# Attention units reordered and paced over half outputs, and one more q through the crossbar, in a sparse-attention and bilinear-FFN kernel

## The chip, the cores and the metric

One core of one Trainium2 chip. The metric is device time in microseconds (us) of one execution. Six runs of the kernel before gave a median of 247.2 us, from 246.9 to 249.48. The profile is of one execution, which took 247.11 us; the span from its first to its last instruction is 245.3 us.

## The reference

Per head, an 8x8 matrix is normalised five times over rows and columns, mixes the eight blocks of k and of v, and each block of q then attends to its own mixed block. The result, with heads side by side, goes through a bilinear FFN.

```python
B, H, S, D = 4, 8, 768, 64          # n_blocks 8, block 96
for _ in range(5):
    P = P - np.max(P, axis=-1, keepdims=True)
    P = np.exp(P)
    P = P / (np.sum(P, axis=-1, keepdims=True) + 1e-09)
    P = P / (np.sum(P, axis=-2, keepdims=True) + 1e-09)
k_sorted = np.einsum('bhij,bhjcd->bhicd', P, k_b)
v_sorted = np.einsum('bhij,bhjcd->bhicd', P, v_b)
scores = scale * q_b @ k_sb.transpose(0, 1, 2, 4, 3)
attn = softmax(scores)
x = (attn @ v_sb).transpose(0, 2, 1, 3).reshape(3072, 512)
out = ((x @ w_a) * (x @ w_b)) @ w_out      # w_a, w_b: 512 x 1536, w_out: 1536 x 512
```

All inputs and the output are float32; the kernel computes in bf16 with float32 sums.

## The kernel before

**Tiling.** Heads go in pairs; pair g = 4*b + hp, so batch b has pairs 4b to 4b+3. A pair's work is a set of units:

- `c_` (a mix unit): where q isn't brought in by the crossbar, `turn_q` (L255) transposes it with 12 matmuls and a copy by DVE; `stage_mix` (L274) mixes k and v, 12 matmuls each, into a two-bank PSUM tile, and copies them to SBUF: kT by two ACT copies, vT by one of DVE and one of ACT. For pairs above the first of batch 1, a DMA transpose on SP's queue then turns vT into vs (L292). For pairs 6 to 13 the unit also issues, on POOL, a tiny `gate` copy that waits for kT (L533) and the three loads of pair g+2 (L95).
- `s_` (a score unit): `stage_scores` (L295), 16 matmuls in two PSUM tiles, each followed by an exp on ACT.
- `o_` (an output unit): `stage_o` (L310), 16 matmuls in two PSUM tiles, each followed on DVE by a reciprocal and a multiply; `to_xT` (L316) then sends the result through a DMA transpose on SP into xT, the FFN's input. It also asks for q of pair g+2: a POOL copy that reorders it (`pair_q`, L244) and a DMA transpose on SP (`stage_q`, L250).

The FFN of a batch is 24 pairs of products (`ffn_ab`, L340: 4 matmuls with w_a, 4 with w_b, an ACT cast and a DVE multiply), 12 for each half of the tokens, and 6 output tiles (`ffn_out`, L368: 12 matmuls, a copy by ACT or DVE, a store on SP).

**Stages.** Sinkhorn's steps run first, on DVE and ACT, while POOL issues loads. Then the first half of batch 0's attention (`half_*` functions) runs alone; the second half is interleaved with the first half of batch 0's FFN. After that, `paced` (L567) interleaves the FFN of batch b with the attention units of batch b+1; the last batch's FFN runs alone. PE, POOL and SP run in program order as written, and so do ACT and DVE in the first stage.

**Pacing.** `paced` runs the FFN's steps and after each issues the units that have fallen due. A pair of products counts 1, an output tile 2; the units are spread evenly up to `spare` output tiles before the end (3 in batch 0, 2 otherwise). Batch 0's FFN has 12 pairs left by then, the others 24.

**Places the change touches.** PSUM is 8 banks: `psA` (L67) has two buffers of two banks, for mixes, scores and o; `psF` (L68) has four of one bank, for FFN tiles and transposes. `replicate` (L434) copies the normalised matrix to `p_rep`, half by DVE and half by POOL; `to_columns` (L439) then turns each half into PSUM columns by matmuls. `begun` (L481) holds the five FFN products of batch 0 started before the last quarter of their input is there: three in psF tiles and two in the halves of one psA tile, `two`. `pair_q(2 * HP - 1)` (L499) reorders q of batch 1's fourth pair; `spread` behind it makes the mixing matrices of batches 2 and 3, also on POOL.

Of the kernel before, what the change touches and what calls it, by code (L numbers as in the profile page):

```python
# [9 lines left out]
FP32 = mybir.dt.float32  # L10
# [6 lines left out]
def _ap(t: bass.AP, extra_offset, pattern):  # L17
    return bass.AP(tensor=t.tensor, offset=t.offset + extra_offset,
                   ap=[list(p) for p in pattern])
# [3 lines left out]
def kernel(  # L23
# [11 lines left out]
    nc = tc.nc  # L35
    P = 128
    B, H, S, D = q.shape
    NB = sort_net.shape[-1]
    BLK = S // NB
    BH = B * H  # L40
    DMODEL = H * D
# [3 lines left out]
    CG = P // NB  # L45
    NCH = S // P
    HP = H // 2
    KA = DMODEL // P
    KO = DFF // P
# [17 lines left out]
    psA = ctx.enter_context(tc.tile_pool(name="psA", bufs=2, space=PSUM))  # L67
    psF = ctx.enter_context(tc.tile_pool(name="psF", bufs=4, space=PSUM))  # L68
# [19 lines left out]
    def load_pair(b, hp):  # L88
        tiles = []
        for name, t in (("k2", k), ("v2", v), ("q2", q)):  # L90
            base = (b * H + 2 * hp) * S * D
            if b == 0 and name == "q2":
                continue
            to = ld.tile([P, 2, W], BF16, tag=name, name=name)
            nc.gpsimd.dma_start(out=to, in_=_ap(t, base, [[W, P], [S * D, 2], [1, W]]))  # L95
            tiles.append(to)
        loaded[b * HP + hp] = tiles
# [3 lines left out]
    w_out_sb = const.tile([P, KO, DMODEL], BF16, name="w_out_sb")  # L101
# [8 lines left out]
    def load_out(c):  # L110
        nc.gpsimd.dma_start(
            out=w_out_sb[:, c * 4:(c + 1) * 4, :],
            in_=moe_w_out.rearrange("(kc p) n -> p kc n", p=P)[:, c * 4:(c + 1) * 4, :])
# [46 lines left out]
    def copy(eng, out, in_):  # L160
        if eng == "act":
            nc.scalar.copy(out=out, in_=in_)  # L162
        else:
            nc.vector.tensor_copy(out=out, in_=in_)  # L164
# [79 lines left out]
    def pair_q(g):  # L244
        qc = qtp.tile([P, NCH, 2, D], BF16, tag="qc", name="qc", bufs=4)
        nc.gpsimd.tensor_copy(out=qc.rearrange("p c e d -> p e c d"),  # L246
                              in_=loaded[g][2].rearrange("p e (c d) -> p e c d", c=NCH))
        st[g, "qc"] = qc

    def stage_q(g):  # L250
        qT = qtp.tile([P, NCH, P], BF16, tag="qTf", name="qTf", bufs=4)
        nc.sync.dma_start_transpose(out=qT, in_=st[g, "qc"].rearrange("p c e d -> p (c e d)"))
        st[g, "qT"] = qT
# [69 lines left out]
    hTs = {}  # L323
# [32 lines left out]
    def ffn_last(b, c):  # L356
        hT = hTs[b]
        rows = out[b * S:(b + 1) * S, :].rearrange("(p c) n -> c p n", c=NCH)
        for n0, n1, eng, queue in ((0, 384, "act", nc.sync), (384, DMODEL, "dve", nc.scalar)):
            po = psF.tile([P, 512], FP32, tag="F", name="po")  # L360
            for m in range(KO):
                nc.tensor.matmul(po[:, 0:n1 - n0], lhsT=hT[:, m, c * P:(c + 1) * P],  # L362
                                 rhs=w_out_sb[:, m, n0:n1], start=(m == 0), stop=(m == KO - 1))
            o_sb = ffp.tile([P, 512], FP32, tag="o_sb", name="o_sb", bufs=3)
            copy(eng, o_sb[:, 0:n1 - n0], po[:, 0:n1 - n0])
            queue.dma_start(out=rows[c][:, n0:n1], in_=o_sb[:, 0:n1 - n0])

    def ffn_out(b, c):  # L368
        if b == B - 1 and c == NCH - 1:
            ffn_last(b, c)  # L370
            return
        hT = hTs[b]
        po = psF.tile([P, DMODEL], FP32, tag="F", name="po")
        for m in range(KO):
            nc.tensor.matmul(po, lhsT=hT[:, m, c * P:(c + 1) * P], rhs=w_out_sb[:, m, :],  # L375
                             start=(m == 0), stop=(m == KO - 1))
        o_sb = ffp.tile([P, DMODEL], FP32, tag="o_sb", name="o_sb", bufs=3)
        copy("act" if c % 2 == 0 else "dve", o_sb, po)
        if b == 0:
            h, u = divmod(c, 3)  # L380
            for c2 in range(2):
                nc.sync.dma_start(
                    out=_ap(out, (h * PH * NCH + 2 * u + c2) * DMODEL,
                            [[NCH * DMODEL, PH], [1, DMODEL]]),
                    in_=o_sb[c2 * PH:(c2 + 1) * PH])
        else:
            rows = out[b * S:(b + 1) * S, :].rearrange("(p c) n -> c p n", c=NCH)
            nc.sync.dma_start(out=rows[c], in_=o_sb)


    with tc.manual_schedule(engines={ET.PE, ET.Pool, ET.SP}):
        with tc.manual_schedule(engines={ET.Activation, ET.DVE}):
            rsum = const.tile([BH, NB], FP32, name="rsum")
            csum = const.tile([BH, NB], FP32, name="csum")
            p_fin = const.tile([BH, NB * NB], FP32, name="p_fin")
            p_rep = const.tile([BH, NB * NB, CG // 2], FP32, name="p_rep")
# [3 lines left out]
            for it in range(5):  # L400
# [8 lines left out]
                if it == 2:  # L409
                    with nc.allow_low_precision("sum of one one and zeros"):  # L410
                        nc.vector.reduce_sum(
                            out=mask, in_=_ap(ident, 0, [[P, P], [1, CG], [CG, NB]]),
# [3 lines left out]
                if it > 0:  # L416
                    nc.tensor.matmul(heat[0:NB, 1, 0:NB], lhsT=rsum, rhs=rsum,
                                     start=True, stop=True)
# [8 lines left out]
                else:  # L427
                    nc.vector.tensor_mul(
                        out=p_fin.bitcast(BF16).rearrange("h (i j u) -> h i j u", i=NB, j=NB),
                        in0=_ap(p_nat, 0, [[NB * NB, BH], [NB, NB], [1, NB], [0, 2]]),  # L430
                        in1=_ap(csum, 0, [[NB, BH], [0, NB], [1, NB], [0, 2]]))
            NR = NBH * NB

            def replicate(eng, hf):  # L434
                eng.tensor_copy(
                    out=p_rep[:, hf * NR:(hf + 1) * NR],
                    in_=_ap(p_fin, hf * NR, [[NB * NB, BH], [1, NR], [0, CG // 2]]))

            def to_columns(hf):  # L439
                for i in range(hf * NBH, (hf + 1) * NBH):  # L440
                    nc.tensor.matmul(
                        pc_ps[:, i, :],
                        lhsT=p_rep[:, i * NB:(i + 1) * NB].bitcast(BF16).rearrange(
                            "h j t -> h (j t)"),
                        rhs=ident[0:BH, 0:BH], start=True, stop=True)

            replicate(nc.vector, 0)
            replicate(nc.gpsimd, 1)
            to_columns(0)
            spread(nc.vector, pc_ps, 0, 2, 0, NBH)  # L450
            spread(nc.vector, pc_ps, 2, 6, 0, NBH)
# [27 lines left out]
            half_x(0, 2, "act")  # L479
            half_o(0, 3)  # L480
            begun = [psF.tile([P, 512], FP32, tag="F", name="pf") for _ in range(3)]  # L481
            two = psA.tile([P, 2, 512], FP32, tag="A", name="two")
            begun += [two[:, 0], two[:, 1]]
            for n, (m, w_sb) in enumerate(((0, w_a_sb), (0, w_b_sb), (1, w_a_sb),
                                           (1, w_b_sb), (2, w_a_sb))):
                if n == 3:
# [9 lines left out]
        load_pair(1, 3)  # L496
        for c in range(3):
            load_out(c)
        pair_q(2 * HP - 1)  # L499
        for g in range(2, 4):  # L500
            spread(nc.gpsimd, p_col, g * 8, 8)
# [22 lines left out]
        def units_full(b):  # L524
            g0, us = b * HP, []

            def c_(g):
                if g < 2 * HP - 1:
                    turn_q(g)
                stage_mix(g, "k", ("act",))  # L530
                stage_mix(g, "v", ("dve", "act"))
                if 2 * HP - 2 <= g < B * HP - 2:
                    nc.gpsimd.tensor_copy(out=gate, in_=kTs[g % NBUF][0:1, 0:1])  # L533
                    load_pair((g + 2) // HP, (g + 2) % HP)

            def s_(g):
                stage_scores(g)
                if g == HP:
                    turn_v(g)
                if g == HP + 1:  # L540
                    stage_q(2 * HP - 1)

            def o_(g):
                stage_o(g)
                to_xT(g)
                if 2 * HP <= g + 2 < B * HP:
                    pair_q(g + 2)
                    stage_q(g + 2)

            for n in range(HP + 1):  # L550
                if n < HP:
                    us.append(lambda g=g0 + n: c_(g))
                    us.append(lambda g=g0 + n: s_(g))
                if n > 0:
                    us.append(lambda g=g0 + n - 1: o_(g))
            return us

        def interleave(steps, units, spare, slow=0):
# [6 lines left out]
                    done += 1  # L565

        def paced(ab, po, units, spare):  # L567
            steps = [(1, f) for f in ab] + [(2, f) for f in po]
            total = sum(t for t, f in steps) - 2 * spare
            now = done = 0  # L570
            for t, step in steps:
                step()
                now += t
                while done < len(units) and done * total < now * len(units):
                    units[done]()
                    done += 1

        steps = [lambda: ffn_ab(0, 0, 0, begun[0:2]), lambda: ffn_ab(0, 1, 0, begun[2:4]),
                 lambda: ffn_ab(0, 2, 0, begun[4:5])]
# [3 lines left out]
        for b in range(B):  # L583
            ab = [lambda m=m, t=t, b=b: ffn_ab(b, m, t)
                  for m in range(KO) for t in range(2) if b > 0 or t == 1]
            po = [lambda c=c, b=b: ffn_out(b, c) for c in range(NCH)]
            paced(ab, po, units_full(b + 1) if b + 1 < B else [], 3 if b == 0 else 2)


# [28 lines left out]
```

The softmax here doesn't subtract the row's maximum and nothing guards it: scores larger than these inputs give would overflow.

## Time and profile before

| what | value |
|---|---|
| median of 6 runs | 247.2 us |
| the profiled execution | 247.11 us |
| its span | 245.3 us |
| granted TensorE clock | 1.00 |
| first pf of batch 0, 1, 2, 3 (FFN) | 21.5, 86.6, 141.1, 195.7 us |
| matmuls of 128x384 into pf (L332) | 760, 77.8 + 77.4 us busy |
| output matmuls of 128x512 (L375) | 60.5 us busy |
| bytes moved | 27.82 MB, about 200 GB/s to 50 us, mean 113 |

Times in the trace are from the span's start. Engines are PE (matmuls), PEld (weight loads, which overlap), DVE, ACT, POOL and SP; a line such as L332 is the line of the kernel. Where an engine sat idle before an instruction, square brackets give how long and what ended the wait. In the chain that ended last, the work is followed back from the last instruction, at each step to what released it. Some matmul records are missing, so a group may count 11 where 12 ran.

### The profile page before, as it was taken

Reading aid. Unit: us, or ns where it says so; the run is one execution under the profiler, and the core shown is the slowest. Engines: PE = TensorE matmul, PEld = TensorE weight load, DVE = VectorE, ACT = ScalarE, POOL = GpSimd, SP = SyncE. Lnnn points to the kernel's source line nnn. Section 1 sums busy time; section 2 is a strip of 40 time slices with the busy share of each in tenths; the row PEclk is TensorE's granted clock in tenths of the full one; section 3 lists DMA queues with packets and bytes.
Section 4 is the critical chain, followed back from the end, with each engine's and each line's share of the span. In section 5 each row is a group of like instructions: output and inputs, shape, how many; then the busy total and the mean of one; then the engine's idle time right before and its main releaser. Section 6 shows DMA issues by size and latency. Waiting matters only on the chain.

```text
span 245.3 us, 5508 instructions
## 1 busy us (share of the span) xinstructions
PE 236.6 (96%) x2246; PEld 137.4 (56%) x2258; DVE 109.2 (45%) x259; ACT 104.1 (42%) x203; POOL 61.0 (25%) x88
## 2 busy tenths in 40 slices
PE   7889899999989999999999999999999999999995
PEld 2466666666644456666645466666645465565443
DVE  6765466556425243464616144454516144443210
ACT  3565764465650046555440055555540033333001
POOL 8885577700332031314141032210000000000000
DMA  6999999946959968939393936935333310000122
GB/s 80 202 199 197 197 200 201 207 76 78 156 96 213 144 134 131 139 68 139 67 168 103 214 73 112 139 65 45 64 90 118 118 45 0 0 3 1 43 106 108
DMA packets 53129, 27.82 MB, mean 113 GB/s; under 512 B 29936, under 2 KB 50160, under 8 KB 53104
## 3 DMA queue, kind: packets, MB, share of 16 engines
q0 software_dynamic: 20944, 14.16, 40.9%
q1 hardware_dynamic: 32016, 13.25, 24.8%
q8 instruction: 17, 0.28, 0.5%
q14 instruction: 8, 0.07, 0.1%
q10 hardware_dynamic: 144, 0.07, 0.1%
HBM read 28.32 MB, written 6.29 MB: 141 GB/s over the span
## 4 chain that ended last, share of the span: by engine, by line
PE 91%; DMA 2%; POOL 2%; DVE 2%; issue 1%; ACT 0%
PE pf L332 51%; PE po L375 24%; PE mix L281 4%; PE o_ps L231 3%; DMA q_first<-in_q_dram 2%; PE sc L302 2%; PE mixh L180 2%; PE po L362 1%; PE vs_ps L208 1%; PE xt_ps L222 1%; PE sc L195 1%; POOL w_b_sb L106 1%; POOL w_a_sb L106 1%; PE two L332 1%; PE q_ps L260 1%
## 5 line engine op out<-in xcount | busy, mean ns | idle before, releaser
L353 DVE TENSOR_TENSOR hT<-a_sb,pf 128x384 bf16<-128x384 bf16 x95 | 52.6, 553 | 73.6 <-PE pf L332 48.5
L332 PE MATMUL pf<-xT,w_a_sb 128*128 128x384 bf16 x380 | 77.8, 326 | 0.0
L332 PE MATMUL pf<-xT,w_b_sb 128*128 128x384 bf16 x380 | 77.4, 326 | 0.0
L352 ACT CAST a_sb<-pf 128x384 bf16<-128x384 f32 x95 | 45.5, 479 | 62.1 <-PE pf L332 40.8
L375 PE MATMUL po<-w_out_sb,hT 128*128 128x512 bf16 x265 | 60.5, 379 | 0.7 <-issue 0.2
L332 PEld LDWEIGHTS <-w_b_sb 128*128 128x128 bf16 x384 | 37.5, 98 | 25.2 <-issue 0.6
L332 PEld LDWEIGHTS <-w_a_sb 128*128 128x128 bf16 x384 | 34.9, 98 | 22.2
L375 PEld LDWEIGHTS <-hT 128*128 128x128 bf16 x276 | 26.3, 98 | 30.3
L162 ACT COPY o_sb<-po 128x512 f32<-128x512 f32 (+1 forms) x13 | 7.5, 578 | 50.3 <-PE po L375 48.9
L164 DVE COPY o_sb<-po 128x512 f32<-128x512 f32 (+1 forms) x12 | 7.9, 658 | 44.3 <-PE po L375 38.7
L307 ACT ACTIVATE eT<-sc 96x768 bf16<-96x768 f32 x24 | 18.1, 803 | 3.2 <-PE sc L302 3.2
L533 POOL COPY gate<-kT 1x1 bf16<-1x1 bf16 x8 | 1.4, 179 | 69.5 <-ACT kT L162 69.5
L237 DVE TENSOR_TENSOR xp<-o_ps,rec 96x512 bf16<-96x512 f32 x24 | 15.7, 683 | 0.2
L162 ACT CAST kT<-mix 128x384 bf16<-128x384 f32 x24 | 10.3, 483 | 8.1 <-PE mix L281 8.1
L95 POOL DMA_DIRECT2D k<-in_k_dram x16 | 11.6, 726 | 5.0 <-PE pf L332 2.0
L95 POOL DMA_DIRECT2D v<-in_v_dram x16 | 11.5, 721 | 2.5 <-DMA w_b_sb<-in_moe_w_b_dram 0.8
L231 PEld LDWEIGHTS <-eT 96*128 96x128 bf16 x256 | 10.3, 97 | 3.1 <-issue 0.6
L246 POOL COPY qc<-q 128x768 bf16<-128x768 bf16 x9 | 7.6, 841 | 16.1 <-DMA q<-in_q_dram 16.1
L231 PE MATMUL o_ps<-vs,eT 96*128 96x65 bf16 x256 | 11.2, 193 | 0.1
L95 POOL DMA_DIRECT2D q<-in_q_dram x12 | 8.7, 723 | 1.6 <-DMA w_a_sb<-in_moe_w_a_dram 0.7
L168 PE MATMUL heat<-warm 128*128 128x512 bf16 x20 | 7.1, 491 | 1.4 <-DVE warm L77 1.3
L164 DVE CAST vT<-mix 128x384 bf16<-128x384 f32 x12 | 6.7, 558 | 3.9 <-PE mix L281 3.8
(80 smaller groups left out, 153.6 us busy)
## 6 DMA issues: line engine op xcount, KB each, us to landing
out_dram<-o_sb SPq DMA_DIRECT2D x17, 256.0 KB, 2.0
k<-in_k_dram POOLq DMA_DIRECT2D x16, 192.0 KB, 5.0
v<-in_v_dram POOLq DMA_DIRECT2D x16, 192.0 KB, 6.1
q<-in_q_dram POOLq DMA_DIRECT2D x12, 192.0 KB, 6.0
w_a_sb<-in_moe_w_a_dram POOLq DMA_DIRECT2D x6, 256.0 KB, 10.4
w_b_sb<-in_moe_w_b_dram POOLq DMA_DIRECT2D x6, 256.0 KB, 10.1
w_out_sb<-in_moe_w_out_dram POOLq DMA_DIRECT2D x3, 512.0 KB, 10.0
out_dram<-o_sb SPq DMA_DIRECT2D x12, 128.0 KB, 2.4
```

The source lines that it names most:

```text
L95: nc.gpsimd.dma_start(out=to, in_=_ap(t, base, [[W, P], [S * D, 2], [1, W]]))
L162: nc.scalar.copy(out=out, in_=in_)
L164: nc.vector.tensor_copy(out=out, in_=in_)
L231: nc.tensor.matmul(o_ps[:, e, i * (D + 1):(i + 1) * (D + 1)], lhsT=eT[:, hf, e, i * BLK:i * BLK + P], rhs=vs[0:BLK, i0 + i, V0 - 1 + e * ( ...
L237: nc.vector.tensor_tensor(out=_ap(xp, i0 * 2 * D, [[nxp * 2 * D, BLK], [D, 2], [2 * D, NBH], [1, D]]), in0=_ap(o_ps, 1, [[1024, BLK], [511 ...
L246: nc.gpsimd.tensor_copy(out=qc.rearrange("p c e d -> p e c d"), in_=loaded[g][2].rearrange("p e (c d) -> p e c d", c=NCH))
L281: nc.tensor.matmul(mix[e * D:(e + 1) * D, c // 3, c % 3 * P:(c % 3 + 1) * P], lhsT=src2[:, e, c * D:(c + 1) * D], rhs=s_all[:, 2 * g + e], ...
L307: nc.scalar.activation(out=eT[:, hf, :, 0:HB], in_=sc[0:BLK, :, 0:HB], func=AF.Exp, scale=float(scale))
L332: nc.tensor.matmul(pf[:, 0:HW], lhsT=w_sb[:, kc, m * P:(m + 1) * P], rhs=x_cols(b, kc, t), start=(kc == 0), stop=(kc == KA - 1))
L352: nc.scalar.copy(out=a_sb, in_=pf[:, 0:HW])
L353: nc.vector.tensor_mul(out=hT[:, m, t * HW:(t + 1) * HW], in0=a_sb, in1=ab[1][:, 0:HW])
L375: nc.tensor.matmul(po, lhsT=hT[:, m, c * P:(c + 1) * P], rhs=w_out_sb[:, m, :], start=(m == 0), stop=(m == KO - 1))
```

## The change

It has five parts. The second half of `p_rep` is copied by ACT in place of POOL. The two products of `begun` that shared the tile `two` get a tile each. In `paced`, output tiles are cut into two steps of 6 matmuls each, and all steps count 1. The units of a batch come in a new order, in which the third and fourth mix stand one unit sooner, before the first and second output unit:

```
before: c0 s0 c1 s1 o0 c2 s2 o1 c3 s3 o2 o3
after:  c0 s0 c1 s1 c2 o0 s2 c3 o1 s3 o2 o3
```

And q of batch 1's third pair (g = 6) goes through POOL's reordering and the crossbar, not through matmuls; with it, q of the pairs from 8 on is asked for in the score unit of the pair before, where the output unit of the second pair before did it.

```diff
--- before.py
+++ after.py
@@ -367,13 +367,21 @@
 
     def ffn_out(b, c):
         if b == B - 1 and c == NCH - 1:
-            ffn_last(b, c)
-            return
-        hT = hTs[b]
-        po = psF.tile([P, DMODEL], FP32, tag="F", name="po")
-        for m in range(KO):
-            nc.tensor.matmul(po, lhsT=hT[:, m, c * P:(c + 1) * P], rhs=w_out_sb[:, m, :],
-                             start=(m == 0), stop=(m == KO - 1))
+            return [lambda: ffn_last(b, c)]
+        held = {}
+
+        def part(n):
+            if n == 0:
+                held["po"] = psF.tile([P, DMODEL], FP32, tag="F", name="po")
+            for m in range(n * KO // 2, (n + 1) * KO // 2):
+                nc.tensor.matmul(held["po"], lhsT=hTs[b][:, m, c * P:(c + 1) * P],
+                                 rhs=w_out_sb[:, m, :], start=(m == 0), stop=(m == KO - 1))
+            if n == 1:
+                store(b, c, held["po"])
+
+        return [lambda: part(0), lambda: part(1)]
+
+    def store(b, c, po):
         o_sb = ffp.tile([P, DMODEL], FP32, tag="o_sb", name="o_sb", bufs=3)
         copy("act" if c % 2 == 0 else "dve", o_sb, po)
         if b == 0:
@@ -432,9 +440,8 @@
             NR = NBH * NB
 
             def replicate(eng, hf):
-                eng.tensor_copy(
-                    out=p_rep[:, hf * NR:(hf + 1) * NR],
-                    in_=_ap(p_fin, hf * NR, [[NB * NB, BH], [1, NR], [0, CG // 2]]))
+                copy(eng, p_rep[:, hf * NR:(hf + 1) * NR],
+                     _ap(p_fin, hf * NR, [[NB * NB, BH], [1, NR], [0, CG // 2]]))
 
             def to_columns(hf):
                 for i in range(hf * NBH, (hf + 1) * NBH):
@@ -444,8 +451,8 @@
                             "h j t -> h (j t)"),
                         rhs=ident[0:BH, 0:BH], start=True, stop=True)
 
-            replicate(nc.vector, 0)
-            replicate(nc.gpsimd, 1)
+            replicate("dve", 0)
+            replicate("act", 1)
             to_columns(0)
             spread(nc.vector, pc_ps, 0, 2, 0, NBH)
             spread(nc.vector, pc_ps, 2, 6, 0, NBH)
@@ -479,8 +486,7 @@
             half_x(0, 2, "act")
             half_o(0, 3)
             begun = [psF.tile([P, 512], FP32, tag="F", name="pf") for _ in range(3)]
-            two = psA.tile([P, 2, 512], FP32, tag="A", name="two")
-            begun += [two[:, 0], two[:, 1]]
+            begun += [psA.tile([P, 2, 512], FP32, tag="A", name="two")[:, 0] for _ in range(2)]
             for n, (m, w_sb) in enumerate(((0, w_a_sb), (0, w_b_sb), (1, w_a_sb),
                                            (1, w_b_sb), (2, w_a_sb))):
                 if n == 3:
@@ -496,6 +502,7 @@
         load_pair(1, 3)
         for c in range(3):
             load_out(c)
+        pair_q(2 * HP - 2)
         pair_q(2 * HP - 1)
         for g in range(2, 4):
             spread(nc.gpsimd, p_col, g * 8, 8)
@@ -525,7 +532,7 @@
             g0, us = b * HP, []
 
             def c_(g):
-                if g < 2 * HP - 1:
+                if g < 2 * HP - 2:
                     turn_q(g)
                 stage_mix(g, "k", ("act",))
                 stage_mix(g, "v", ("dve", "act"))
@@ -537,22 +544,19 @@
                 stage_scores(g)
                 if g == HP:
                     turn_v(g)
-                if g == HP + 1:
-                    stage_q(2 * HP - 1)
+                if g in (HP, HP + 1):
+                    stage_q(g + 2)
+                if 2 * HP <= g + 1 < B * HP:
+                    pair_q(g + 1)
+                    stage_q(g + 1)
 
             def o_(g):
                 stage_o(g)
                 to_xT(g)
-                if 2 * HP <= g + 2 < B * HP:
-                    pair_q(g + 2)
-                    stage_q(g + 2)
-
-            for n in range(HP + 1):
-                if n < HP:
-                    us.append(lambda g=g0 + n: c_(g))
-                    us.append(lambda g=g0 + n: s_(g))
-                if n > 0:
-                    us.append(lambda g=g0 + n - 1: o_(g))
+
+            for u, n in ((c_, 0), (s_, 0), (c_, 1), (s_, 1), (c_, 2), (o_, 0), (s_, 2), (c_, 3),
+                         (o_, 1), (s_, 3), (o_, 2), (o_, 3)):
+                us.append(lambda u=u, g=g0 + n: u(g))
             return us
 
         def interleave(steps, units, spare, slow=0):
@@ -565,12 +569,11 @@
                     done += 1
 
         def paced(ab, po, units, spare):
-            steps = [(1, f) for f in ab] + [(2, f) for f in po]
-            total = sum(t for t, f in steps) - 2 * spare
-            now = done = 0
-            for t, step in steps:
+            steps = ab + po
+            total = len(steps) - 2 * spare
+            done = 0
+            for now, step in enumerate(steps, 1):
                 step()
-                now += t
                 while done < len(units) and done * total < now * len(units):
                     units[done]()
                     done += 1
@@ -583,7 +586,7 @@
         for b in range(B):
             ab = [lambda m=m, t=t, b=b: ffn_ab(b, m, t)
                   for m in range(KO) for t in range(2) if b > 0 or t == 1]
-            po = [lambda c=c, b=b: ffn_out(b, c) for c in range(NCH)]
+            po = [f for c in range(NCH) for f in ffn_out(b, c)]
             paced(ab, po, units_full(b + 1) if b + 1 < B else [], 3 if b == 0 else 2)
 
 
```

## The prediction

> **What bounds the kernel now.** I read the page first: busy times, the chain, the groups.
>
> ```profile
> PE 236.6 (96%) x2246; PEld 137.4 (56%) x2258; DVE 109.2 (45%) x259; ACT 104.1 (42%) x203; POOL 61.0 (25%) x88
> ```
>
> PE is busy for 236.6 of 245.3 us, no other engine for half of it, and the chain that ended last is 91% PE. The granted clock is 1.00 in every 5 us window, so PE time falls only by taking matmuls away or by closing gaps. The gaps are 245.3 - 236.6 = 8.7 us. The chain in order of time (start, length, what) shows which can be closed:
>
> ```profile
> 13.13 0.41 POOL p_rep L435
> 13.54 0.04 issue
> 13.59 0.26 PE pc_ps L441 x4
> ...
> 26.33 0.55 DVE hT L353
> 26.87 0.04 issue
> 26.91 0.32 PE two L332
> ...
> 59.89 0.46 PE q_ps L260 x12
> 60.35 0.67 PE mix L281 x24
> ...
> 69.96 0.81 PE mix L281 x24
> 70.80 0.57 DVE vT L164
> 71.39 0.49 ACT vT L162
> 71.88 0.04 issue
> 71.92 0.35 PE sc L302 x8
> 72.26 0.16 issue
> ...
> 87.90 0.79 PE mix L281 x24
> ```
>
> Three places lie off PE inside the body: PE waits for a POOL copy at 13.5, for a DVE multiply at 26.3, and for copies of a mix at 70.8. The rest of the 8.7 us is the first copies, Sinkhorn's serial steps and the last store, which the change leaves alone. The timeline has the first gap from both sides:
>
> ```profile
> 11.21 0.28 DVE L435 COPY p_rep<-p_fin 32x256 f32<-32x256 f32 x1
> ...
> 13.59 0.26 PE L441 MATMUL pc_ps<-ident,p_rep 32*128 32x32 bf16 x4 [0.83 <-POOL p_rep L435]
> ```
>
> DVE copied its half at 11.21; POOL, first in issuing weight loads, reached the other half at 13.13. The reader should see that p_fin had been ready since 11.18.
>
> **Part 1: second half of p_rep from POOL to ACT.** ACT's queue ahead of it is two qT copies, over at 11.13. Its nearest copies by size are 0.26 us (32x64 exp) and 0.48 us (128x384 cast), so this one ends by 11.18 + 0.48 = 11.7. Behind it on ACT stands the kT cast, which started at 12.60. PE wants the data after the v half-mix, 13.59 - 0.83 = 12.76. The whole 0.83 us goes, if nothing is late next. Next are: the heads 2 to 7 of s_all (DVE ready 12.60, wanted 13.0), kT (13.08, wanted 13.3), vT (13.35, wanted 13.6), p_col behind vT (13.35 + 0.42 = 13.8, then the vs copy at 14.0). Pairs of k and v land about 1 us apart; POOL's next issues, which wait for those landings, put v2 before 15.07 (its half-mix would come at 16.66 - 0.83 = 15.83) and k3 before 15.80 (16.47). All hold, with 0.2 us at the narrowest, so I take 0.80; bounds 0.5 (one of the narrow ones is 0.3 late) to 0.83.
>
> **Part 2: "two" as two tiles.** The last matmul into the second half waited 0.61 us until DVE had read the first half: one tile, two banks. With two tiles that reader is no longer waited for. Price: both psA buffers are held. The second takes the buffer of the last o_ps, which DVE has read by 22.61 with PE there at 23.6 (and the xph transposes between wait for the same DVE work anyway). The next sc takes the first one's buffer, free at 26.87, wanted at 27.89 - 0.61 = 27.28. What is late next is ACT's a_sb of that step, behind two casts until 27.07 instead of 27.27; four psF buffers cover it. I take 0.58; bounds 0.4 to 0.61.
>
> **Part 3: q of pair 6 by the crossbar.** Off PE go 12 transposes, off DVE one qT copy of 0.55, which hid behind PE. With q_ps ahead, q_ps and mix take 0.46 + 0.67 = 1.13; the mix of a pair without them takes 0.79 (87.90). So 0.34 us, not 0.46; bounds 0.34 and 0.46. Added: one POOL copy (mean 0.84) ahead of pair 7's copy and two spreads. It waits for q of pair 6, and pair 7's copy, behind it, waited 3.49 us for its own later load until 44.76, which hides it; without that cover the spreads end 0.84 later than 49.5 and are first needed at 87.9. On SP it adds a transpose (1.24 to issue, median 2.8 to landing) at about 42 to 46, wanted at 63. Cost zero.
>
> A rule here. The trace has 12 transposes in 0.46 us, 0.04 each. "TensorE: Matmul & The Clock Gate" (Part 4, PE-mode transpose) gives about 275 ns for one in a kernel. By that, my estimate of this part would be 12 x 0.275 = 3.3 us and the forecast some 3 us lower; the row decides against it.
>
> **Part 4: units over output halves.** In batch 0's FFN the steps are 12 pairs and then 12 half outputs (before, 6 outputs that count 2), and the 12 units are spread over the first 18, so they fall due past 0, 1.5, 3, ... steps. Before, the fourth mix and its scores both fell due after the first output tile: PE went mix, wait, scores. After, the mix comes at step 11, scores at 14, half an output past the first half, so its three casts (kT twice, vT) are hidden by 3.9 us of matmuls. The stage from 67.37 to 86.60 is 19.23 us; its work is 6 outputs x 2.59 (67.37 to 69.96) + mix 0.79 + scores 0.45 + two o units x 0.49 = 17.76. Excess 1.47 us. What may come back: the last o (step 17) follows the one before (step 16) by one half output, 1.29 us, and DVE must first copy the second output. Before, from that output's end (74.96) DVE was through both halves of the first o at 77.11, 2.15 us later. The second half of the last o would want its buffer at 0.49 + 1.29 + 0.25 = 2.03. So 0.2 us with latency. Its vs by the crossbar: from the end of the mix to the last o I add 1.41 + 1.29 + 0.49 + 1.29 + 0.45 + 2.59 + 0.49 + 1.29 = 9.3 us; against it 1.1 to 1.6 for the casts and 3.0 to 6.4 to land:
>
> ```profile
> vs<-vT SPq DMA_TRANSPOSE x11, 5.6
> ```
>
> That is 8.0 at worst. I take 1.47 - 0.2 = 1.27; bounds 0.65 (only the longest stall goes) and 1.47.
>
> A rule against this part. All windows have clock 1.00, also where units stand between FFN steps. The same page ("Why this matters for your kernels") wants all K-tiles of a thin product run together, lest the clock oscillate. By it, an estimate: the six halved outputs of one batch at half clock would cost 6 x 2.59 = 15.5 us more. But units put matmuls, no idle time, between the halves.
>
> **Part 5: mixes one unit sooner in batches 2 and 3, q later.** Before, these stages had no gap (86.60 to 195.66 is PE piece on piece), so there is nothing to win. The third and fourth mix go from steps 14 and 22 to 11 and 19; o 0 and 1 from 11 and 19 to 14 and 22; the last o stays at 30, so xT lands as before. With each mix go its gate and three loads on POOL and the vs transpose on SP, all earlier and so safer. q of pair g+1 is now asked for at scores g, one (mix, scores) ahead where it was two. Tightest is pair 9: gate to 89.2, loads to 92.43, copy 0.85 gives 93.3, landing 2.8 (most 4.5) gives 96.1 (97.8); scores start at 100.65. On SP it stands behind vs of pair 8, issued at 89.83. Zero, with bounds 0.1 gained and 0.6 lost.
>
> **The sum.** 0.80 + 0.58 + 0.34 + 1.27 = 2.99. Profiled span 245.3 - 3.0 = 242.3; around it lie 247.11 - 245.3 = 1.81, giving 244.1. The profiled run is 0.09 under the median 247.2, so against the median 244.2. I say 244.1. The lower bounds sum to 0.5 + 0.4 + 0.34 + 0.65 - 0.6 = 1.3 (245.9), the upper to 0.83 + 0.61 + 0.46 + 1.47 + 0.1 = 3.5 (243.7).
>
> **Rivals.**
> A: the forecast, 244.1, chance 0.70, its own range 243.6 to 245.2.
> B: the early gains are swallowed, since to 50 us the loads run at a steady 200 GB/s and PE can't outrun them. Then only 0.34 + 1.27 count: 245.6. For it: the DMA row is full there. Against: no wait of PE on a load stands in the chain after 13.6. Chance 0.12.
> C: the change moves the wait. psA has two buffers; close o units or scores wait for DVE or ACT, and part 4 gives back its 1.27 and some of the early parts: about 246.3. For it: the last o is now one half behind its neighbour. Against: 0.2 by the rows. Chance 0.10.
> D: slower. The q transposes on SP's in-order queue, asked for late, arrive after their scores are due. Place: scores of pairs 9 and 13, six steps after the request. From q landing 100.65 - 93.3 = 7.4 us after its copy, each microsecond more stalls PE fully, twice. To lose 3.0 and another 1.3 each must be 2.15 late, a landing of 9.5 us: 248.5 and up. For it: vs landed after up to 6.4 us. Against: q never over 4.5. Chance 0.08.
>
> **The numbers.** A kernel like this tells about 0.5% from no change: 1.24 us, so faster is under 245.96. A and B are faster but for a tail of 0.04 where their losses add up: 0.78; C and that tail same, 0.14; D 0.08. Range: 243.5, past A's upper bounds, to 246.0, which takes in B and leaves out D and most of C.
>
> **What would show it.** Right: PE's wait on p_rep is gone from the list of waits, "two" waits for no hT, the sequence mix, vT, scores is gone and the stage from the first output to the next batch's first pf is near 17.9 us, with 12 q_ps fewer. Wrong: a wait of scores on qTf, of o_ps on vs or xp, of pf on weights, or pieces in batches 2 and 3 longer than 54.5 us from one batch's first pf to the next (86.60 to 141.13).

## The result and the profile after

| | before, beside it | after |
|---|---|---|
| median | 247.91 us (49 runs, 246.86 to 253.39) | 246.06 us (23 runs, 245.52 to 246.60) |
| ratio, 95% interval | | 0.9929 [0.9911, 0.9947] |
| profiled execution | 247.11 us | 246.82 us |
| its span | 245.3 us | 245.1 us |

The kernel is 0.71% faster (0.53 to 0.89). That is about 1.75 us of 247.8, where 3.0 were forecast. Before's median of 247.91 stands above the 247.2 shown earlier because 19 of its 49 executions took 249 us or more, and the ratio leaves out only the longest of these: the median of the other 30 is 247.24 us, 1.18 above after's.

The profiled execution of after is the longest of its kernel (other spans: 243.7 to 244.8). The changed kernel was run again as the first experiment, with a span of 244.3 us, and where one execution's luck matters I read that one too.

The page of after has the engines' busy times, and PE's list of waits, from its second line on, has the total in us, the count and the longest:

```profile
PE 237.0 (97%) x2234; PEld 137.2 (56%) x2246; DVE 109.4 (45%) x258; ACT 104.5 (43%) x204; POOL 61.3 (25%) x88
```

```profile
PE sc L195 <- issue: 0.9, 1, 0.9
PE pc_ps L448 <- DVE p_rep L164: 0.5, 1, 0.5
...
PE o_ps L231 <- DVE xp L237: 0.2, 1, 0.2
```

The waits that the change was to remove are gone: no wait on POOL's p_rep, none of "two" on hT, none of scores on vT. PE has 12 matmuls fewer. But the line of scores on "issue" is new. Scores of the first stage wait 0.9 us for nothing that the profile shows. The chain of after, in order of time (start, length, what), has the three places of the prediction and the last copy:

```profile
18.16 0.23 PE sc L195 x6
18.39 0.87 issue
19.26 0.22 PE sc L195 x2
...
26.79 0.50 PE mixh L180 x24
27.29 0.27 PE two L332
...
70.84 0.29 PE sc L302 x8
71.15 0.34 PE sc L302 x8
...
85.89 1.30 PE pf L332 x8
...
241.74 0.29 DVE o_sb L164
```

PE stops in the middle of 8 matmuls whose operands are there: six run, two come 0.87 us later. "two" follows the mixes at once. The four-step jam of mix, vT, scores at 70 is gone. And from the end of DVE's last copy, at 242.03, to the end of the span is 3.1 us; before, it was 242.75 to 245.3, 2.55:

```profile
242.46 0.29 DVE o_sb L164
```

### The profile page after: what moved, and what is told of

Same layout as the page of the kernel before. It is cut to its first block, busy times and chain, and to the rows that moved or that the text cites. A ratio compares the mean times of both kernels' runs of the same rounds, so it can differ in the third digit from the quotient of the medians.

```text
span 245.1 us, 5487 instructions
## 1 busy us (share of the span) xinstructions
PE 237.0 (97%) x2234; PEld 137.2 (56%) x2246; DVE 109.4 (45%) x258; ACT 104.5 (43%) x204; POOL 61.3 (25%) x88
## 4 chain that ended last, share of the span: by engine, by line
PE 92%; DVE 4%; issue 1%; ACT 1%; DMA 1%
PE pf L332 51%; PE po L377 24%; PE mix L281 4%; PE o_ps L231 3%; PE sc L302 2%; PE mixh L180 2%; PE po L362 1%; PE vs_ps L208 1%; PE sc L195 1%; PE xt_ps L222 1%; PE heat L168 1%; DMA p_nat<-in_sort_net_dram 1%; PE q_ps L260 1%; PE two L332 1%; DVE xp L237 1%
## 5 line engine op out<-in xcount | busy, mean ns | idle before, releaser
L377 PE MATMUL po<-w_out_sb,hT 128*128 128x512 bf16 x265 | 61.3, 379 | 0.6
L237 DVE TENSOR_TENSOR xp<-o_ps,rec 96x512 bf16<-96x512 f32 x24 | 15.9, 684 | 0.6 <-DVE rec L235 0.2
L235 DVE RECIPROCAL rec<-o_ps 96x8 f32<-96x8 f32 x32 | 5.6, 189 | 13.8 <-PE o_ps L231 13.8
L246 POOL COPY qc<-q 128x768 bf16<-128x768 bf16 x10 | 8.4, 840 | 7.5 <-DMA q<-in_q_dram 7.5
L168 PE MATMUL heat<-warm 128*128 128x512 bf16 x20 | 7.7, 529 | 1.4 <-DVE warm L77 1.3
```

Of the source, the lines that this page charges most:

```text
L168: nc.tensor.matmul(ps[:, 0:cols], lhsT=warm[:, 0:P], rhs=warm[:, 0:cols], start=True, stop=True)
L237: nc.vector.tensor_tensor(out=_ap(xp, i0 * 2 * D, [[nxp * 2 * D, BLK], [D, 2], [2 * D, NBH], [1, D]]), in0=_ap(o_ps, 1, [[1024, BLK], [511 ...
L377: nc.tensor.matmul(held["po"], lhsT=hTs[b][:, m, c * P:(c + 1) * P], rhs=w_out_sb[:, m, :], start=(m == 0), stop=(m == KO - 1))
```

## The experiments

Every kernel was run beside the kernel before. Medians of five or more runs, ratios with 95% intervals. There are three groups of four experiments, in the order below, with medians of the kernel before of 247.46, 247.54 and 247.62 us. The change itself ran only in the first, so a later median is set against it across groups, and a difference of 0.1 to 0.2 us says nothing.

**The change again.**

> The changed kernel once more. Theory F: the 0.87 us gap of PE in the middle of the half scores of pair 2 (18.39 in the first profile) is PE waiting for its next block of instructions, asked for a fixed number of instructions earlier while the loads fill the DMA engines; it comes back in every execution, 0.6 to 1.1 us long, in the same place. Rival R: it is an accident of one execution, and the part on p_rep really gave its 0.8; then the gap is gone here, and the time is about 245.3. The start (p_fin at 11.18 before, 11.83 after) may differ by half a us from execution to execution under both.

Measured: 245.91 us, ratio 0.9932 [0.9908, 0.9956], span 244.3. Its chain:

```profile
12.94 0.19 PE pc_ps L448 x4
...
17.40 0.23 PE sc L195 x6
17.64 0.87 issue
18.51 0.22 PE sc L195 x2
```

The gap comes again, of the same size, after the same six matmuls, though everything here runs 0.75 us earlier than in the first profile. So it is neither luck nor a fixed time; it sits at a fixed place in PE's program. In the trace of after, 222 matmuls and 224 weight loads lie ahead of the two that come late. The DMA queue's rows name a candidate. In the stretch from 16 to 17 us of this execution (packets, MB, share of the 16 engines):

```profile
q0 software_dynamic: 371, 0.18, 136.2%
q8 instruction: 1, 0.02, 5.9%
```

One packet of instructions, among 371 packets of loads; it is the first of its queue in the span. Over the whole span there are 17 such packets with 0.28 MB, 16 KB each.

**Undo the first part: p_rep's second half on POOL again.**

> The changed kernel with the second half of p_rep on POOL again. F: PE waits about 0.8 us for p_rep again, between the request for the block and its use, so the gap in the scores of pair 2 goes and the time stays within 0.3 us of the changed kernel. R: no gap in either, the wait comes back alone, 0.6 to 0.9 us slower.

```diff
-            replicate("act", 1)
+            nc.gpsimd.tensor_copy(out=p_rep[:, NR:2 * NR],
+                in_=_ap(p_fin, NR, [[NB * NB, BH], [1, NR], [0, CG // 2]]))
```

Measured: 245.85 us, 0.9931 [0.9902, 0.9961], span 244.1: no different from the change. Its timeline, with the idle time before an instruction in brackets:

```profile
13.14 0.41 POOL L455 COPY p_rep<-p_fin 32x256 f32<-32x256 f32 x1
...
13.61 0.26 PE L448 MATMUL pc_ps<-ident,p_rep 32*128 32x32 bf16 x4 [0.63 <-DVE vT L164]
...
18.07 0.37 PE L195 MATMUL sc<-qT,kT 64*128 64x96 bf16 x8
```

The wait at 13.6 is back (the last to release it shows as vT; POOL's copy ended 0.06 us before) and the gap at 18 is gone: the eight scores run in one piece. The first part of the change moves a wait, it removes none.

**Move the border of PE's instructions.** If PE waits for a block of instructions, the block should be asked for sooner when PE is further on in its program at the same time. Warming matmuls of 512 columns were cut into two of 256: same PE time, 21 matmuls and 21 weight loads more ahead of the gap. The same edit to the kernel before is the control.

> The changed kernel with the warming matmuls of the start cut in two (256 columns, twice as many): about 42 more PE instructions (21 pairs) ahead of the same work, the same columns. F: the block's border moves 42 instructions up the program, its request falls into the wait for Sinkhorn and comes 1 to 2 us sooner; the gap of 0.87 goes or falls under 0.2, 0.6 to 0.9 us faster than the changed kernel. R: no difference beyond 0.2 us, or slower by the added weight loads.

> The kernel before with the same 42 more instructions, as a control. F: no gap was left in it (the block arrived 0.1 us ahead of its use), so the time is that of the kernel before within 0.2 us. R: the same; should the added instructions themselves cost or bring something, it shows here.

```diff
-            keep_busy(heat[:, 0], 8)
+            keep_busy(heat[:, 0], 16, 256)
...
-                    keep_busy(heat[:, 0], (0, 4, 3, 2, 4)[it])
+                    keep_busy(heat[:, 0], (0, 8, 6, 4, 8)[it], 256)
```

Measured: in after, 245.02 us, 0.9887 [0.9845, 0.9928], span 243.9; that is 0.89 us faster than the change itself. In before, 247.30 us, 0.9996 [0.9963, 1.0028]: nothing. The chain of the edit in after:

```profile
13.46 0.19 PE pc_ps L448 x4
...
17.93 0.28 PE sc L195 x8
```

The eight scores run in one piece. Its first instruction packet starts at 13.2 us (13.4 in the control), against 16.0 in the change run again, 16.8 in after, 15.9 with POOL's copy and 15.7 before. Over the span, the queue now carries 18 packets in place of 17, so it is PE's:

```profile
q8 instruction: 18, 0.29, 0.5%
```

So the gap is PE's wait for its own instructions, its price is the whole 0.9 us, and it had been hidden under the wait on p_rep: with POOL's copy, PE reaches that place just as the block arrives. The rest of the record agrees: each of the nine profiles with the copy on ACT and the old border has the gap, 0.55 to 0.90 us long, and the five with the copy on POOL or the border moved have none.

**The first part alone, in the kernel before.**

> The kernel before with one edit, the second half of p_rep on ACT. F: the wait of 0.83 goes, and a gap of 0.5 to 0.9 us appears in the half scores of pair 2, where PE waits for its block of instructions; the fastest executions are within 0.3 us of those of the kernel before. R: 0.6 to 0.9 us faster, no gap. A third thing to look at: so far the kernels with this copy on POOL had executions of 249 to 253 us among the others, those with it on ACT none over 246.8; if the copy is the cause, this one has none either.

Measured: 247.21 us, 0.9986 [0.9967, 1.0005], span 245.5. Its chain:

```profile
17.45 0.23 PE sc L195 x6
17.69 0.55 issue
18.23 0.22 PE sc L195 x2
```

The same place, the same stop after six. Of the 0.83 us, 0.55 come back here, and PE's waits have a further new line, where an output unit of batch 1 waits for vs from the crossbar:

```profile
PE o_ps L231 <- DMA vs<-vT: 0.3, 1, 0.3
```

Alone, the first part gains nothing that is clear of zero.

**Undo the second part: one tile "two" again.**

> The changed kernel with the two products in one tile again. F: the wait of PE for hT before the last matmul into the second half comes back, 0.4 to 0.6 us slower. R (the saving was made up elsewhere, since loads run at a fixed rate to 50 us): within 0.15 us.

```diff
-            begun += [psA.tile([P, 2, 512], FP32, tag="A", name="two")[:, 0] for _ in range(2)]
+            two = psA.tile([P, 2, 512], FP32, tag="A", name="two")
+            begun += [two[:, 0], two[:, 1]]
```

Measured: 246.59 us, 0.9948 [0.9920, 0.9976], 0.5 to 0.7 us behind the change. PE's waits have the old line again, beside the 0.9 us of the gap:

```profile
PE two L332 <- DVE hT L353: 0.6, 1, 0.6
```

The second part is worth its 0.6 us although PE has just waited for instructions.

**Undo the third part: q of the third pair by matmuls again.**

> The changed kernel with q of pair 6 by matmuls again, so one DMA fewer on SP. By PE alone it is 0.34 us slower. Theory T on the tail: from the end of DVE's last copy to the end of the span it took 2.6 us in the kernel before and 3.05 in every kernel with the change; the wait at the end goes over the eight semaphores of SP's and ACT's DMAs in order, and the one more DMA moved the last store from the last of them to the first, with seven more checks behind it. T: here the tail is 2.6 again, so the time is 0.1 us faster to 0.05 slower. Rival: the tail belongs to something else in the change and stays at 3.05; 0.3 to 0.4 us slower.

```diff
-        pair_q(2 * HP - 2)
...
-                if g < 2 * HP - 2:
+                if g < 2 * HP - 1:
                     turn_q(g)
...
-                if g in (HP, HP + 1):
+                if g == HP + 1:
                     stage_q(g + 2)
```

Measured: 246.13 us, 0.9940 [0.9918, 0.9961], span 243.9. On PE the part is worth what was forecast. From the second group of pc_ps (L448) to batch 1's first pf it is 12.94 to 85.13 in the change run again, 72.19 us with a gap of 0.87; here it is 12.88 to 85.18, 72.30 us with a gap of 0.64. Without the gaps that is 71.32 against 71.66: 0.34. What pays it back is at the other end of the trace. DVE's last copy here, and SP's wait for the last store (total, count, longest):

```profile
241.02 0.29 DVE L164 COPY o_sb<-po 128x128 f32<-128x128 f32 x1 [4.46 <-PE po L362]
```

```profile
SPq L615 <- DMA out_dram<-o_sb: 1.1, 1, 1.1
```

against the change run again:

```profile
240.98 0.29 DVE L164 COPY o_sb<-po 128x128 f32<-128x128 f32 x1 [4.46 <-PE po L362]
```

```profile
SPq L616 <- DMA out_dram<-o_sb: 1.7, 1, 1.7
```

From the end of the last copy to the end of the span is 243.9 - 241.31 = 2.59 us with q by matmuls, and 244.3 - 241.27 = 3.03 with q by the crossbar. The tail is 0.44 us longer for one DMA more on SP, issued 190 us earlier. The medians, 246.13 and 246.06, don't tell the two kernels apart.

**Shift the last store once more.** The theory for the tail: at the end SP waits for the DMAs' 8 semaphores in a fixed order, the DMAs take these in turn, and one DMA more puts the last store on another of them. Four stores cut in two move it four on.

> The changed kernel with the first four stores of the last batch cut in two, four more DMAs on SP while its queue is idle. T: the last store moves four semaphores on, four checks fewer behind it, a tail of 2.75 to 2.85 in place of 3.05, 0.2 to 0.3 us faster. Rival: the tail stays at 3.05 and the time within 0.1 us.

```diff
+            if b == B - 1 and c < 4:
+                for r in range(2):
+                    nc.sync.dma_start(out=rows[c][r * PH:(r + 1) * PH],
+                                      in_=o_sb[r * PH:(r + 1) * PH])
+            else:
                 nc.sync.dma_start(out=rows[c], in_=o_sb)
```

Measured: the tail is 244.0 - 241.26 = 2.74 us, as the theory had it, and SP's wait 1.4 us. The semaphore records of the traces show the order itself. SP's and ACT's DMAs, 64 with q by matmuls and 65 with the change, go to 8 semaphores in turn, and near the end of its program SP checks these in a fixed order, 0.06 us apart. In the change run again the last store lands on the first of them, at 242.95, and the check of the eighth starts at 243.40; with q by matmuls it lands on the eighth, at 242.99, and that check starts at 243.01. From this last landing to the end of the span it is 1.34 us against 0.93. The median of 246.05 us, 0.9938 [0.9912, 0.9964], is not the 0.2 to 0.3 us lower that was expected. The tail's cause is thus shown; that a shorter tail shortens the run is not shown by this kernel.

**The fourth part, halves and order apart.** First the new order of units with whole outputs as steps, then the old order with half outputs.

> The changed kernel, its new order kept, paced by whole outputs as before. Theory P: what closed the gap between the fourth mix and its scores is the mix's new place, two FFN steps earlier; the halves add little. Then the stage from the first output to the next batch's first pf (18.14 us with the change, 19.23 before) stays within 18.0 to 18.8 (o and scores now stand side by side and share the two psA buffers), and the time is 0.1 faster to 0.6 us slower. Rival: the halves do it; the stage is 19.0 or more and the time 0.9 us slower or more.

```diff
-            steps = ab + po
+            steps = [(1, [f]) for f in ab]
+            steps += [(2, po[i:i + 2]) for i in range(0, len(po), 2)]
```

> The changed kernel, paced over halves, with the units in their old order. One half output (1.3 us) stands between the fourth mix and its scores, against 1.3 to 1.5 us for the copies between them. P: the halves alone would nearly do as well; within 0.4 us of the changed kernel. Rival: only the new order closes the gap; 0.7 us slower or more. In batches 2 and 3 (54.5 us each from first pf to first pf) no difference under either.

```diff
-            for u, n in ((c_, 0), (s_, 0), (c_, 1), (s_, 1), (c_, 2), (o_, 0), (s_, 2), (c_, 3),
-                         (o_, 1), (s_, 3), (o_, 2), (o_, 3)):
-                us.append(lambda u=u, g=g0 + n: u(g))
+            for n in range(HP + 1):
+                if n < HP:
+                    us.append(lambda g=g0 + n: c_(g))
+                    us.append(lambda g=g0 + n: s_(g))
+                if n > 0:
+                    us.append(lambda g=g0 + n - 1: o_(g))
```

Measured: 247.11 us, 0.9982 [0.9954, 1.0010], and 246.73 us, 0.9962 [0.9942, 0.9982]. Either half of the fourth part alone is behind both together, by 1.05 and 0.67 us against the change's 246.06; for the second this lies between the two expectations. PE's waits and the chain of the first:

```profile
PE sc L302 <- DVE xp L237: 1.3, 2, 0.8
```

```profile
70.66 0.70 DVE xp L237
71.35 0.05 issue
71.40 0.34 PE sc L302 x8
```

With whole outputs, o and scores fall due together. Scores want the two psA buffers that o has just filled, and DVE needs 0.69 us for each multiply. My theory that the order alone brings the time is wrong. The chain of the second:

```profile
67.79 0.79 PE mix L281 x24
68.58 1.14 PE po L377 x5
69.72 6.42 DMA vs<-vT
76.14 0.14 issue
76.28 0.65 PE o_ps L231 x16
```

With the old order the last mix comes so shortly before the last o that vs, issued at 69.72 and 6.42 us in the crossbar, holds up this o by 1.4 us. In neither does PE still wait for the copies of the mix: each edit alone closes the old gap and opens another. From the first output to batch 1's first pf the two take 19.08 and 19.50 us, the change 18.14, the kernel before 19.23.

**Take DVE's copy out of the way of the last o.**

> The changed kernel with the copy of batch 0's second output on ACT in place of DVE. In the trace of the change the last o waited for DVE, which copied that output first (0.69 us). Theory: the wait of o_ps for xp goes, the stage falls from 18.14 to 17.8 to 17.9, 0.2 to 0.35 us faster. Rival: the buffers or vs from the crossbar hold PE anyway; within 0.1 us.

```diff
-        copy("act" if c % 2 == 0 else "dve", o_sb, po)
+        copy("act" if c % 2 == 0 or (b, c) == (0, 1) else "dve", o_sb, po)
```

Measured: 245.95 us, 0.9936 [0.9918, 0.9955], the same as the change.

```profile
75.31 0.70 DVE xp L237
76.00 0.05 issue
76.05 0.42 PE o_ps L231 x8
```

The last o still waits, now for DVE's own multiply of the o before it. The stage is 18.03 us against 18.14: 0.11 us came of it.

**Border moved, ACT's copy, and seven late stores cut in two, together.**

> The changed kernel with three edits: the warming matmuls cut in two (F: 0.9 us), the copy on ACT (0.3), and seven more stores by cutting seven late ones in two, which puts the last store on the semaphore that it had in the kernel before (T: a tail of 2.6, 0.45 us). Sum: 245.9 - 1.65 = 244.3, 244.0 to 244.7. If the three hinder each other or one of the theories is wrong, 244.9 or more.

```diff
+            if c + 6 * b in (16, 17, 18, 19, 20, 21, 22):
```

Measured: 244.83 us (244.75 to 244.97), 0.9889 [0.9869, 0.9909], span 243.2. This is the best version, 1.2 us ahead of the change, though 0.1 to 0.5 us short of what I expected. Among PE's waits none of scores on "issue" is left, and the tail is 243.2 - 240.67 = 2.53 us. Most of the 1.2 us is the border: that edit alone gave 245.02. The copy and the shorter tail thus gave some 0.2 us together, across two groups, where 0.75 were expected of them.

## Why the prediction was wrong

The kernel is faster, and by less than forecast. Point by point:

**Part 1 (0.80 forecast, about 0 in the time).** This is the step that failed. The prediction says: "The whole 0.83 us goes, if nothing is late next." Its list of what is next has the heads of s_all, kT, vT, p_col and the landings of k and v; it leaves out PE's own instructions. The wait of 0.83 us went, ACT's copy took 0.40 us as bounded, and 0.87 us came back five microseconds later because PE's next block of instructions was late. The packet starts at 16.0 us without the p_rep wait (the change run again) and at 15.9 with it (POOL's copy), so PE must ask for it ahead of that wait, and a faster PE behind it brings nothing. The gap ends 2.2 to 2.5 us after the packet's start in all nine profiles that have it, as in after (16.8, 19.26), in the change again (16.0, 18.51) and in the first part alone (15.9, 18.23). Undoing the part costs nothing, moving the border returns 0.9 us. Rival B had this effect for this part, an early gain swallowed while loads fill the queue, but put it on data; and it was wrong on the second part, whose 0.6 stayed.

The Trainium skill bears on this gap. "Runtime: NRT & Kernel Launch" (Instruction fetch mechanics) says that instructions are refilled in blocks of 16 KiB by a DMA queue and that this is mostly hidden. The 0.28 MB in 17 packets agree with the block; but it is not hidden here, at 0.87 us.

**Part 2 (0.58 forecast, 0.6 shown).** Right, in its mechanism and its size.

**Part 3 (0.34 forecast).** The matmuls went and nothing waited for q of the third pair; the whole stretch on PE fits 0.34. "Cost zero" for the added transpose on SP was wrong, in a place where I didn't look: one DMA more moved the last store to another of the semaphores that the end waits for, and the tail grew from 2.55 to 3.03 us, by 0.4 to 0.5. The medians show no gain from the part: the change is at 246.06, the kernel without it at 246.13. No term of the sum stood for the tail.

**Part 4 (1.27 forecast, 0.79 shown).** Right in its mechanism, off in size. The window of after from batch 0's first output to batch 1's first pf has its length, the busy time of PE, PEld, DVE, ACT and POOL, the granted clock, the DMA share and GB/s:

```profile
67.75:85.89 18.14, 17.77 (x135) 8.79 (x136) 6.67 (x15) 3.25 (x6) 2.42 (x4) 1.00 0.83 159
```

The stage is 18.14 us. The mix is no longer in it, so its work is 6 outputs x 2.59 + scores 0.45 + three o units x 0.49 = 17.46. The excess is 0.68 where before it was 1.47, so 0.79 is gained, and not 1.27, because I let only the last o wait, 0.2 us. It waits 0.33; the second half of the scores waits another 0.2, by DVE's row for the buffer of the o before (its multiply ends at 71.10, they start at 71.15), and 0.11 lie behind the scores. Rival C named such waits on the two psA buffers; they took a third of the part, not all of it. That the measured median lies nearest to C's 246.3 is luck: by C part 4 loses all of its 1.27, and it lost 0.48; the rest went in part 1 and in the tail, for other reasons. The sign "near 17.9 us" in the prediction kept the stage's old work of 17.76; with the mix out and an o in, its own sum gives 17.46 + 0.2 = 17.66, so 18.14 is 0.48 above it and not 0.2. The granted clock is 1.00 in every 5 us window of after too: the halves cost no clock. The two half experiments add that both are needed: halves without the order, or the order without halves, don't shorten the stage by more than 0.15 us.

**Part 5 (0 forecast, 0 shown).** From one batch's first pf to the next it is 85.89, 140.41, 194.93: 54.52 us twice, against 54.53 before. Rival D, late q on SP, did not happen: no wait on qTf is among PE's waits.

**The sum, for the change run again.** Part 1 gives 0, part 2 0.6, part 3 0.34, part 4 0.79; against them 0.45 for the tail, as the traces show it, and 0.11 for one more passage from mix to pf. That is 1.2, and the spans fell by 245.3 - 244.3 = 1.0, in an execution whose first stage began 0.18 us later. The forecast's 2.99 lost 0.80 in part 1, 0.48 in part 4 and 0.45 in the tail. Against the 247.2 of the six runs shown before, the median of 246.06 is 1.14 us less, and 1.18 less than the 247.24 given with the result, which is about this sum.

## What to carry to other kernels

When a wait is removed early in a kernel that is still loading, ask what else arrives by DMA at that point, and put the engine's own instructions on the list: a gap in the middle of equal matmuls whose operands are there, put down to "issue", is its mark, and it can be moved by where the block's border falls. An overlap bought with one more DMA can be paid for at the end of the kernel (0.44 us of the span here), so compare the tail (last copy to end of span) too. And price a reordering by which buffers the neighbouring steps hold, and test its halves alone, since here each half closed the old gap and opened a new one.

## What the runs showed of the hardware

- **PE's instructions come by DMA, and a block can be late.** Loads moved about 200 GB/s while the packet that ends the gap was due; 42 more instructions ahead of it brought its start from 16.0 to 13.2 us. At which instruction PE asks, and how long the packet then queues, no run measured. That the loads are to blame is not shown: the packet itself took 0.95 us, and the mean of all 17 in that trace is 1.14.
- **DVE's small copy took 0.28 us or 0.58.** Half of p_rep, 32x256, is the same copy in every kernel. Before, it began at 11.21, ahead of POOL's next DMA issue, and took 0.28 us. In after it began during one:

```profile
11.60 0.74 POOL L106 DMA_DIRECT2D w_a_sb<-in_moe_w_a_dram  x1 [0.26 <-DMA k<-in_k_dram]
11.85 0.40 ACT L162 COPY p_rep<-p_fin 32x256 f32<-32x256 f32 x1
11.85 0.58 DVE L164 COPY p_rep<-p_fin 32x256 f32<-32x256 f32 x1
```

  PE's wait on p_rep, 0.2 us before and in the change run again, is 0.5 in after for this; in the change run again, where the copy began 0.03 us before POOL's issue, it took 0.28. In seven of the 14 profiles the copy began 0.25 to 0.50 us into an issue; it took 0.33 to 0.58 us and always ended 0.83 us after that issue's start. In the other seven it began between issues, or 0.12 us into one, and took 0.28. "SBUF — State Buffer" of the Trainium skill (Who interferes with whom) says that DVE's faster modes and GpSimd share a port pair and that the one which comes second waits. These rows fit such a wait; that a port is its cause no run here tested.
- **The start differs from execution to execution.** p_fin ended at 11.18 us before, at 11.83 in after and 11.36 in the change run again, all with a granted clock of 1.00. The four warming matmuls that start at 5.0 us took 1.22, 1.89 and 1.60 us; the eight before them took 3.6 us in all three. The instructions up to this point are the same in the three, so up to 0.65 us between two single profiles need not be the effect of an edit.
